# Half of the second chunk's first layer between parts of the first chunk's second layer, with the second group's joins and the third chunk's state later

## The chip, the cores and the metric

One core of one Trainium2 chip. The metric is the time of the kernel on the device in microseconds (us); lower is better. All timed runs here are of the fast state (for one single look the state is unknown). The kernel before took 670.79 us (median of 6 runs beside the changed kernel; 670.61 to 671.75).

## The reference, cut to what matters

```python
# deltanet: 4 batches x 8 heads, 768 steps, head size 48
for t in range(S):
    y[:, :, t] = einsum('bhd,bhde->bhe', q[:, :, t], state)
    v_old = einsum('bhde,bhd->bhe', state, k_n[:, :, t])
    state = state + b_t * einsum('bhd,bhe->bhde', k_n[:, :, t], v_t - v_old)
# then a feed-forward layer with exact Gelu, 3072 tokens
x = y.transpose(0, 2, 1, 3).reshape(B * S, H * D)      # 3072 x 384
return gelu(x @ w_in) @ w_out                          # 384 -> 2048 -> 384, w_* are float64 inputs
```

The kernel cuts the 768 steps into 12 chunks of 64. A group is two chunks. For a group VectorE eliminates a small triangular system ("elimination"), TensorE and VectorE join its halves ("joins"), then each chunk's state step gives x, its transpose xT, and the feed-forward work on it. The weights arrive as 64-bit floats and are decoded to 32 bits by integer work on VectorE and ScalarE.

## The kernel before: the parts that matter

The order of work is a plan. Each step has a time in units of one chunk of feed-forward work; steps are emitted in that order. VectorE keeps the emitted order (the kernel emits this plan under manual_schedule for VectorE alone); the queues of the other engines are ordered by a scheduler that follows it.

```python
    def back(x):                                  # end of the elimination: VectorE transposes
        if x == 0: transpose(XM <- Nu)            # L453
        else:                                     # L457: x == 1 right columns, x == 2 left columns
            transpose(Zf[:, :, cols] <- Nu)
        if x == 2:                                # clear two quarter blocks of Zf
            ...nc.scalar.mul / nc.gpsimd.memset   # L464, L466
    # ... cut ...
    def fc1(c, f):                                # first layer, one of 16 blocks of hidden units
        psH = ps.tile([128, NA * 128], F32, tag="mlp", name="psH")
        for m in range(NM):
            nc.tensor.matmul(psH, lhsT=w_in_sb[...], rhs=xTs[c][:, m, :], ...)
        nc.scalar.activation(G[:, f, :], psH, ACT.Gelu)

    def fc2(u, f0, f1):                           # second layer, four blocks f of one half of the tokens
        if f0 == 0: u.psO = ps.tile([128, DM], F32, tag="mlp", name="psO")
        for f in range(f0, f1):
            nc.tensor.matmul(u.psO, lhsT=G[:, f, ...], rhs=w_out_sb[:, f, :], ...)
    # ... cut ...
    ones = [(1.3, fc1, c, f) for f in range(NF)]
    twos = [(2.7, fc2, tiles[c, a], f, f + 4) for a in range(NA) for f in range(0, NF, 4)]
    if c == 0: twos.sort(key=lambda s: s[3])
    return ones + twos
    # ... cut ...
    plan = [at(c + 1, c + 2, ffn_steps(c)) for c in range(NC)]
    plan += [at(0.985, 1.26, decode_steps(3, n_in)), at(1.26, 1.65, decode_steps(n_in, NW)), ...]
    plan += [..., at(1.75, 2.45, eliminate_steps(1)),
             at(2.58, 2.74, join_steps(1)), at(2.72, 2.98, state_steps(2)), ...]
```

join_steps(1) are three steps: the first makes psJ from XM and G for the third chunk, and VectorE multiplies it into XM; the second makes the other half of the third chunk from Zf and the new XM, together with the first half of the fourth chunk; the third makes the rest.

Of the kernel before, what the change touches and what calls it, by code (L numbers as in the profile page):

```python
# [16 lines left out]
def kernel(  # L17
# [33 lines left out]
    NC = S // C  # L51
# [370 lines left out]
    def eliminate_steps(g):  # L422
        steps = []

        def scales():
            gt = wk.tile([128, HB], F32, tag="gt", name="gt", bufs=1)
            gl = XMs[g] = wk.tile([128, NU, HB], F32, tag="XM", name="XM", bufs=1)
            nc.vector.transpose(gt, gms[g].rearrange("q t h -> q (t h)"))
            nc.gpsimd.tensor_tensor(gl, low, gt.unsqueeze(2).to_broadcast([128, HB, HB]),
                                    op=ALU.mult)  # L430

        def flip():
            Nus[g] = wk.tile([128, HB, HB], F32, tag="Nu", name="Nu", bufs=1)
            nc.vector.transpose(Nus[g], Ds[g].rearrange("q u n -> q n u"))
            nc.vector.tensor_tensor(Nus[g], Nus[g], XMs[g], op=ALU.mult)

        def eliminate(j):
            nu = Nus[g]
            n = HB - 1 - j
            tmp = wk.tile([128, HB * HB // 4], F32, tag="tmp", name="tmp")  # L440
            tmp = tmp[:, 0:n * j].rearrange("q (i c) -> q i c", i=n)
            nc.vector.tensor_tensor(tmp, nu[:, j + 1:, j:j + 1].to_broadcast([128, n, j]),  # L442
                                    nu[:, j:j + 1, 0:j].to_broadcast([128, n, j]), op=ALU.mult)
            nc.vector.tensor_tensor(nu[:, j + 1:, 0:j], nu[:, j + 1:, 0:j], tmp, op=ALU.add)  # L444

        def diagonal():
            flat = Nus[g].rearrange("q i c -> q (i c)")
            nc.vector.memset(flat[:, 0:HB * HB:HB + 1], 1.0)

        def back(x):  # L450
            nu = Nus[g]
            if x == 0:
                nc.vector.transpose(XMs[g].rearrange("q u c -> q c u"),  # L453
                                    nu.rearrange("q i c -> q c i"))
            else:
                cols = slice(HB, C) if x == 1 else slice(0, HB)
                nc.vector.transpose(Zf[g % 2][:, :, cols].rearrange("q u i -> q i u"), nu)  # L457
            if x == 2:
                for cc in range(2):
                    for p in range(2):  # L460
                        part = Zf[g % 2][p * C + HB:(p + 1) * C,
                                         cc * NU // 2:(cc + 1) * NU // 2, 0:HB]
                        if g == cc == p == 0:
                            nc.scalar.mul(part, low[0:HB, 0:HB // 2], 0.0)  # L464
                        else:
                            nc.gpsimd.memset(part, 0.0)  # L466

        steps = [(0.3, scales), (3.0, flip)]
        steps += [(0.7, eliminate, j) for j in range(1, HB - 1)]
        steps += [(0.1, diagonal)]  # L470
        steps += [(1.9, back, x) for x in range(3)]
        return steps

    def join(g, ts, level, copy=nc.scalar.copy):

        xm, zf, off = XMs[g], Zf[g % 2], Gs[g]
        gm = gms[g].rearrange("q t h -> q (t h)")
        psJ = dn("psJ").rearrange("q b (u n) -> q b u n", n=HB)
        for i, u in enumerate(range(ts[0] * H, (ts[-1] + 1) * H)):
            for p in range(2):  # L480
                top = slice(p * C, p * C + HB)
                low_ = slice(p * C + HB, (p + 1) * C)
                rows, to = (top, low_) if level == 0 else (low_, top)
                nc.tensor.matmul(psJ[to, i // (2 * H), i % (2 * H), :],
                                 lhsT=(xm if level else off)[rows, u, :],
                                 rhs=zf[rows, u, HB:C] if level else xm[rows, u, :],
                                 start=True, stop=True)
        for i in range(0, len(ts), 2):
            us = slice(ts[i] * H, (ts[min(i + 1, len(ts) - 1)] + 1) * H)
            n = us.stop - us.start  # L490
            for p in range(2):
                top = slice(p * C, p * C + HB)
                low_ = slice(p * C + HB, (p + 1) * C)
                if level == 0:
                    nc.vector.tensor_tensor(
                        xm[low_, us, :], psJ[low_, i // 2, 0:n],
                        gm[low_, us].unsqueeze(2).to_broadcast([HB, n, HB]), op=ALU.mult)
                else:
                    copy(zf[top, us, HB:C], psJ[top, i // 2, 0:n])
# [43 lines left out]
    def join_steps(g):  # L543
        a, b = range(NA), range(NA, 2 * NA)
        return [(1.0, join_run, g, a, ()), (1.0, join_run, g, b, a), (1.0, join_run, g, (), b)]
# [120 lines left out]


    FH = NF // 2
    DH = DM // 2
    B11, B12 = w_out_sb[:, 0:FH, 0:DH], w_out_sb[:, 0:FH, DH:]  # L670
    B21, B22 = w_out_sb[:, FH:, 0:DH], w_out_sb[:, FH:, DH:]
    T = {}

    def fc1(c, f):
        psH = ps.tile([128, NA * 128], F32, tag="mlp", name="psH")
        for m in range(NM):
            nc.tensor.matmul(psH, lhsT=w_in_sb[:, f // 2, m, f % 2 * 128:(f % 2 + 1) * 128],  # L677
                             rhs=xTs[c][:, m, :], start=(m == 0), stop=(m == NM - 1))
        nc.scalar.activation(G[:, f, :], psH, ACT.Gelu)  # L679
# [112 lines left out]
    def ffn_steps(c):  # L792
        ones = [(1.3, fc1, c, f) for f in range(NF)]
        if c > 1:
            return [(1.3, first_layer, c, f) for f in range(NF)] + [
                (2.6, second_layer, c, n) for n in (1, 5, 2, 6, 4, 7, 3)]
        twos = [(2.7, fc2, tiles[c, a], f, f + 4) for a in range(NA) for f in range(0, NF, 4)]
        if c == 0:
            twos.sort(key=lambda s: s[3])
        return ones + twos  # L800

    def at(first, last, steps):

        total, done, timed = sum(s[0] for s in steps), 0.0, []
        for w, *step in steps:
            timed.append((first + (last - first) * (done + 0.5 * w) / total, step))
            done += w
        return timed
# [32 lines left out]
    signs(0, 2)  # L841
    diagonals(first[3])
    root(n0)
    scales_, flip_, *rows, back0, back1, back2 = [s_[1:] for s_ in eliminate_steps(0)]
    factors(gms[0], beta_m[:, 0:2].rearrange("q c a h -> q (c a) h"), n0)
    scales_[0]()
    flip_[0]()
# [36 lines left out]
    back2[0](*back2[1:])  # L884
    for a in range(NA):
        join(0, (a,), 1)
    for u in first[NA:]:
        scale_v(u)
    begin(0)
# [27 lines left out]
    def late():  # L917
# [3 lines left out]
        for a in range(NA):  # L921
# [3 lines left out]
            for c in range(5, NC, 2):  # L925
                tiles[c, a].Kb = Kb

    plan = [at(c + 1, c + 2, ffn_steps(c)) for c in range(NC)]
    plan += [at(0.985, 1.26, decode_steps(3, n_in)), at(1.26, 1.65, decode_steps(n_in, NW)), at(1.66, 1.67, [(1.0, late)])]
    plan += [at(0.98, 0.985, [(1.0, load, 3)]),  # L930
             at(1.02, 1.1, [(1.0, join, 0, range(NA, 2 * NA), level) for level in range(2)]),
]
    sums = [(1.0, sum_of_squares, tiles[c, a], h) for c in (2, 3) for a in range(NA) for h in range(H)]
    plan += [at(1.08, 1.5, sums), at(1.51, 1.511, [(1.0, prep, c) for c in (2, 3)]), at(1.65, 1.655, [(1.0, finish_both)]), at(2.97, 2.971, [(1.0, finish, 4)]), at(2.675, 2.676, [(1.0, queries, third)]),
             at(1.12, 1.6, state_steps(1)),
             at(1.75, 2.45, eliminate_steps(1)),
             at(2.58, 2.74, join_steps(1)), at(2.72, 2.98, state_steps(2)),
             at(2.67, 2.671, [(1.0, prep, 4)]), at(2.8, 2.9, [(1.0, grams, [tiles[4, a] for a in range(NA)])])]
    plan += [at(0.995, 1.0, [(1.0, load_v, 2)]), at(2.98, 2.981, [(1.0, sums_of_w)]), at(3.1, 3.11, [(1.0, last_sum_of_w)])]
    plan += [at(c - 0.4, c - 0.3, v_steps(c)) for c in range(4, NC)]  # L940
    plan += [at(2.08, 2.44, [(1.0, scale_head, tiles[c, a], h)
# [2 lines left out]
    for c in range(4, NC):  # L944
        us = [tiles[c, a] for a in range(NA)]
        t = {4: 1.8, 5: 2.1}.get(c, c - 2.9)
        plan += [at(t, t + 0.01, [(1.0, load_blocks, c, "Kb", k)])]
        t = 3.2 if c == 4 else c - (1.3 if c % 2 == 0 else 0.9)
        plan += [at(t, t + 0.01, [(1.0, load_blocks, c, "Qb", q)])]
        t = c - (2.1 if c % 2 == 0 else 2.6) if c > 5 else {4: 2.1, 5: 2.69}[c]  # L950
        plan += [at(t, t + 0.01, [(1.0, load_k, c, "Kn")])]
        plan += [at(c - 0.4, c - 0.39, [(1.0, load_k, c, "Kp")])]
        t = {4: 2.73, 5: 2.95}.get(c, c - (1.97 if c % 2 == 0 else 2.36))
        plan += [at(t, t + 0.01, [(1.0, turned_k, u) for u in us])]
        t = c + (0.05 if c % 2 == 0 else -0.34)
        plan += [at(t, t + 0.01, [(1.0, turned_q, u) for u in us])]
# [56 lines left out]
```

## Time and profile before

| what | before |
|---|---|
| time, median of 6 | 670.79 us |
| profiled execution | 671.82 us, span 670.1 us |
| TensorE busy, of the span | 640.3 us, 96% |
| VectorE busy, of the span | 452.3 us, 67% |
| end of weight decoding on VectorE | 117.3 us |
| first layer of the second chunk done | 141.22 us |
| first layer of the third chunk starts | 178.55 us |

The lines behind this table are shown in the prediction. To read them: a row of a timeline has start, length, engine, line, operation, output <- input, count, and in brackets how long the engine sat idle before and what ended it. "x24" records of psH are four steps of the first layer; each step is six records. Only time lost before about 230 us can be won; after that TensorE is busy 436.1 of 440.0 us (230 to 670), and its longest gap before its last record, at 666 us, is 0.12 us.

### The profile page before, as it was taken

How to read it: one execution, taken by the hardware profiler on the slowest of the kernel's cores; microseconds unless marked ns; L12 is line 12 of the kernel's file. 1: busy time of each engine (PE TensorE's matmuls, PEld its weight loads, DVE VectorE, ACT ScalarE, POOL GpSimd, SP SyncE). 2: the span in 40 equal slices, each digit the busy share in tenths (PEclk: the TensorE clock that was granted, in tenths of full speed). 3: DMA queues.
4: the chain of work that ended last, by engine and by line, in shares of the span. 5: the costliest groups of instructions: out<-in, count | busy, mean ns of one | idle time of the engine just before them, and what ended most of it. 6: DMA issues, size and time to landing. Idle time of an engine off the chain costs nothing.

```text
span 670.1 us, 21705 instructions
## 1 busy us (share of the span) xinstructions
PE 640.3 (96%) x9542; PEld 559.4 (83%) x9542; DVE 452.3 (67%) x921; ACT 228.6 (34%) x605; POOL 82.1 (12%) x82
## 2 busy tenths in 40 slices
PE   5767998999999999999999999999999999999997
PEld 4656775866689989989989989989989989989997
DVE  6999999994689846489846479846479844324021
ACT  3357754714342143142143142143142133122220
POOL 4051300103111021111021111021111010000000
PEclk8576999999999999999999999999999999999999
DMA  9785655203431232511332511211401210100101
GB/s 130 174 253 167 121 172 135 48 0 66 81 51 32 53 53 44 82 31 30 55 49 49 84 29 26 53 21 30 68 3 24 55 20 3 24 2 2 24 1 25
DMA packets 158431, 39.76 MB, mean 59 GB/s; under 512 B 150016, under 2 KB 153216, under 8 KB 158336
## 3 DMA queue, kind: packets, MB, share of 16 engines
q1 hardware_dynamic: 152464, 33.40, 26.3%
q10 hardware_dynamic: 5872, 4.97, 3.2%
q8 instruction: 75, 1.23, 0.8%
q14 instruction: 20, 0.16, 0.1%
HBM read 33.62 MB, written 4.72 MB: 57 GB/s over the span
## 4 chain that ended last, share of the span: by engine, by line
PE 82%; DVE 10%; ACT 3%; issue 2%; DMA 2%; SPq 1%; DVEq 0%; ACTq 0%
PE psH L677 36%; PE psX L715 12%; PE psY L715 12%; PE psZ L715 4%; PE psJ L517 3%; PE psK L572 3%; PE psG L367 3%; PE psO L690 2%; PE psU L597 2%; DVE Nu L444 2%; DVE tmp L442 2%; PE psY L615 1%; DVE w_e L235 1%; DVE w_out_sb L236 1%; PE psY L624 1%
## 5 line engine op out<-in xcount | busy, mean ns | idle before, releaser
L677 PE MATMUL psH<-xT,w_in_sb 128*128 128x256 f32 x1152 | 261.5, 383 | 2.3 <-ACT G L679 2.3
L677 PEld LDWEIGHTS psH<-xT,w_in_sb 128*128 128x128 f32 x1152 | 215.6, 190 | 33.7 <-ACT G L679 3.9
L679 ACT ACTIVATE G<-psH 128x256 f32<-128x256 f32 x192 | 73.3, 382 | 180.4 <-PE psH L677 168.3
L444 DVE TENSOR_TENSOR Nu<-Nu,tmp 128x30 f32<-128x30 f32 (+9 forms) x180 | 61.8, 343 | 6.2
L442 DVE TENSOR_TENSOR tmp<-Nu 128x30 f32<-128x30 f32 (+9 forms) x180 | 61.6, 342 | 5.1
L715 PE MATMUL psX<-w_out_sb,G 128*128 128x192 f32 x320 | 56.2, 329 | 0.0
L715 PE MATMUL psY<-w_out_sb,G 128*128 128x192 f32 x304 | 54.1, 329 | 0.6
L715 PEld LDWEIGHTS psX<-w_out_sb,G 128*128 128x128 f32 x320 | 52.2, 190 | 0.7
L715 PEld LDWEIGHTS psY<-w_out_sb,G 128*128 128x128 f32 x304 | 49.1, 190 | 2.1 <-DVE u L761 1.8
L690 PE MATMUL psO<-w_out_sb,G 128*128 128x384 f32 x128 | 45.1, 495 | 1.6 <-DVE w_out_sb L236 1.6
L660 ACT COPY xT<-psX 128x384 f32<-128x384 f32 x24 | 11.3, 476 | 102.9 <-PE psX L659 102.8
L306 POOL TENSOR_TENSOR n<-n,half 128x16 f32<-128x16 f32 x10 | 29.4, 2938 | 87.9 <-DVE n L281 66.9
L690 PEld LDWEIGHTS psO<-w_out_sb,G 128*128 128x128 f32 x128 | 23.1, 190 | 16.9 <-DVE w_out_sb L236 4.0
L603 ACT COPY U<-psU 64x192 f32<-64x192 f32 x96 | 30.0, 313 | 19.5 <-PE psU L597 18.3
L402 DVE TENSOR_TENSOR P<-psG,mask 128x1024 f32<-128x1024 f32 x10 | 12.2, 1224 | 35.6 <-PE psG L367 35.6
L580 DVE TENSOR_TENSOR W<-psK,V 128x384 f32<-128x384 f32 x22 | 12.1, 552 | 29.1 <-ACT y L579 29.0
L466 POOL MEMSET Zf<- 32x512 f32 x23 | 12.4, 541 | 154.5 <-DVE Zf L457 153.6
L724 DVE TENSOR_TENSOR S<-G 128x512 f32<-128x512 f32 x20 | 13.7, 687 | 25.8 <-ACT G L679 25.7
L332 POOL TENSOR_TENSOR V<-V,n 128x384 f32<-128x384 f32 x18 | 17.1, 958 | 106.1 <-DMA V<-in_v_dram 67.6
L638 DVE TENSOR_TENSOR x<-psY,y 64x192 f32<-64x192 f32 x80 | 28.3, 354 | 0.9
L715 PE MATMUL psY<-T,G 128*128 128x192 f32 x160 | 28.2, 329 | 0.0
L715 PE MATMUL psX<-T,G 128*128 128x192 f32 x160 | 28.1, 329 | 0.0
(138 smaller groups left out, 866.9 us busy)
## 6 DMA issues: line engine op xcount, KB each, us to landing
Kp<-in_k_dram SPq DMA_DIRECT2D x76, 96.0 KB, 3.6
w_out_sb<-in_moe_w_in_dram SPq DMA_DIRECT2D x24, 256.0 KB, 4.2
V<-in_v_dram SPq DMA_DIRECT2D x48, 96.0 KB, 2.9
out_dram<-o_sb ACTq DMA_DIRECT2D x46, 96.0 KB, 2.2
w_raw<-in_moe_w_out_dram SPq DMA_DIRECT2D x10, 384.0 KB, 5.4
Zf<-in_moe_w_out_dram SPq DMA_DIRECT2D x6, 384.0 KB, 5.1
Qp<-in_q_dram SPq DMA_DIRECT2D x64, 32.0 KB, 2.2
Qp<-in_q_dram SPq DMA_DIRECT2D x16, 96.0 KB, 4.3
```

Of the source, the lines that this page charges most:

```text
L306: nc.gpsimd.tensor_tensor(flat, flat, half, op=ALU.pow)
L367: nc.tensor.matmul(psG[HALF[p], r, i * NP + j, :], lhsT=u.Kt[rows, p, j, :], rhs=(u.Qt if x else u.Kt)[rows, p, j, :], start=True, stop=True)
L442: nc.vector.tensor_tensor(tmp, nu[:, j + 1:, j:j + 1].to_broadcast([128, n, j]), nu[:, j:j + 1, 0:j].to_broadcast([128, n, j]), op=ALU.mult)
L444: nc.vector.tensor_tensor(nu[:, j + 1:, 0:j], nu[:, j + 1:, 0:j], tmp, op=ALU.add)
L517: nc.tensor.matmul(psJ[to, i, :], lhsT=(xm if level else off)[rows, u, :], rhs=zf[rows, u, HB:C] if level else xm[rows, u, :], start=True, ...
L572: nc.tensor.matmul(u.psK[to, x, r, j, :], lhsT=(u.Qt if x else u.Kt)[rows, p, j, :], rhs=St[rows, u.a, p, j, :], start=True, stop=True)
L603: copy(pairs(u.U[HALF[p]], s), u.psU[HALF[p ^ s], p])
L638: nc.vector.tensor_tensor(dst, src, pairs(u.y[HALF[p ^ s]], s), op=ALU.add)
L677: nc.tensor.matmul(psH, lhsT=w_in_sb[:, f // 2, m, f % 2 * 128:(f % 2 + 1) * 128], rhs=xTs[c][:, m, :], start=(m == 0), stop=(m == NM - 1))
L679: nc.scalar.activation(G[:, f, :], psH, ACT.Gelu)
L690: nc.tensor.matmul(u.psO, lhsT=G[:, f, u.a * 128:(u.a + 1) * 128], rhs=w_out_sb[:, f, :], start=(f == 0), stop=(f == NF - 1))
L715: nc.tensor.matmul(ps_, lhsT=lhs[:, f, :], rhs=rhs[:, f, :], start=first and f == 0, stop=f == FH - 1, skip_group_check=not first)
```

## The change

Its intent: while TensorE waits for decoded second-layer weights of the first chunk, it does half of the second chunk's first layer. TensorE is then ahead, so what follows from VectorE's elimination is put later. Apart from that, two quarter blocks of the first group are cleared after the join copies and not before. The core of the diff:

```diff
-            if x == 2:
+            if x == 2 and g > 0:
+                clear(g)
+        def clear(g): ...                      # as before, for g == 0 called after join(0, (a,), 1)
+    EARLY = 8
     def fc1(c, f):
-        psH = ps.tile([128, NA * 128], F32, tag="mlp", name="psH")
+        if c == 1 and f < EARLY:
+            psH = dn("psH")[:, 0, 0:NA * 128]
+        else:
+            psH = ps.tile([128, NA * 128], F32, tag="mlp", name="psH")
@@ ffn_steps
-        return ones + twos
+            more_ = [(1.3, fc1, 1, f) for f in range(EARLY)]
+            return ones + twos[:-2 * NA] + more_[:4] + twos[-2 * NA:-NA] + more_[4:] + twos[-NA:]
+        return ones[EARLY:] + twos
@@ plan
-    plan = [at(c + 1, c + 2, ffn_steps(c)) for c in range(NC)]
+    plan = [at(c + 1 + 0.25 * (c == 1), c + 2 + 0.25 * (c == 0), ffn_steps(c)) for c in range(NC)]
-    queries of the third chunk at 2.675, joins at(2.58, 2.74), state at(2.72, 2.98), prep 4 at 2.67
+    queries of the third chunk at 2.725, joins at(2.64, 2.77), state at(2.76, 2.985), prep 4 at 2.72
-    load_k 5 at 2.69, turned_k 4 at 2.73 and 5 at 2.95
+    load_k 5 at 2.74, turned_k 4 at 2.76 and 5 at 2.955
```

(The last four lines stand for five lines of the diff in which only these numbers change; other lines are cut.)

More of the change, by code (lines that the diff above doesn't have):

```diff
@@ L457, in back, with clear @@
                 nc.vector.transpose(Zf[g % 2][:, :, cols].rearrange("q u i -> q i u"), nu)
-            if x == 2:
+            if x == 2 and g > 0:
+                clear(g)
+        def clear(g):
                 for cc in range(2):
@@ L471, in eliminate_steps @@
         steps += [(1.9, back, x) for x in range(3)]
-        return steps
+        return steps + [(0.0, clear, 0)] if g == 0 else steps
     def join(g, ts, level, copy=nc.scalar.copy):
@@ L843 @@
     root(n0)
-    scales_, flip_, *rows, back0, back1, back2 = [s_[1:] for s_ in eliminate_steps(0)]
+    scales_, flip_, *rows, back0, back1, back2, clear_ = [s_[1:] for s_ in eliminate_steps(0)]
     factors(gms[0], beta_m[:, 0:2].rearrange("q c a h -> q (c a) h"), n0)
@@ L886 @@
         join(0, (a,), 1)
+    clear_[0](*clear_[1:])
     for u in first[NA:]:
@@ L933 @@
     sums = [(1.0, sum_of_squares, tiles[c, a], h) for c in (2, 3) for a in range(NA) for h in range(H)]
-    plan += [at(1.08, 1.5, sums), at(1.51, 1.511, [(1.0, prep, c) for c in (2, 3)]), at(1.65, 1.655, [(1.0, finish_both)]), at(2.97, 2.971, [(1.0, finish, 4)]), at(2.675, 2.676, [(1.0, queries, third)]),
+    plan += [at(1.08, 1.5, sums), at(1.51, 1.511, [(1.0, prep, c) for c in (2, 3)]), at(1.65, 1.655, [(1.0, finish_both)]), at(2.97, 2.971, [(1.0, finish, 4)]), at(2.725, 2.726, [(1.0, queries, third)]),
              at(1.12, 1.6, state_steps(1)),
              at(1.75, 2.45, eliminate_steps(1)),
-             at(2.58, 2.74, join_steps(1)), at(2.72, 2.98, state_steps(2)),
-             at(2.67, 2.671, [(1.0, prep, 4)]), at(2.8, 2.9, [(1.0, grams, [tiles[4, a] for a in range(NA)])])]
+             at(2.64, 2.77, join_steps(1)), at(2.76, 2.985, state_steps(2)),
+             at(2.72, 2.721, [(1.0, prep, 4)]), at(2.8, 2.9, [(1.0, grams, [tiles[4, a] for a in range(NA)])])]
     plan += [at(0.995, 1.0, [(1.0, load_v, 2)]), at(2.98, 2.981, [(1.0, sums_of_w)]), at(3.1, 3.11, [(1.0, last_sum_of_w)])]
@@ L949 @@
         plan += [at(t, t + 0.01, [(1.0, load_blocks, c, "Qb", q)])]
-        t = c - (2.1 if c % 2 == 0 else 2.6) if c > 5 else {4: 2.1, 5: 2.69}[c]
+        t = c - (2.1 if c % 2 == 0 else 2.6) if c > 5 else {4: 2.1, 5: 2.74}[c]
         plan += [at(t, t + 0.01, [(1.0, load_k, c, "Kn")])]
         plan += [at(c - 0.4, c - 0.39, [(1.0, load_k, c, "Kp")])]
-        t = {4: 2.73, 5: 2.95}.get(c, c - (1.97 if c % 2 == 0 else 2.36))
+        t = {4: 2.76, 5: 2.955}.get(c, c - (1.97 if c % 2 == 0 else 2.36))
         plan += [at(t, t + 0.01, [(1.0, turned_k, u) for u in us])]
```

## The prediction

> **What bounds the kernel now.** I read the page first, then the chain of waits, then TensorE's own order of work, then busy time by stage. The page has TensorE at 96% of the span, and its second part shows that what is missing is at the start.
>
> ```profile
> PE   5767998999999999999999999999999999999997
> DVE  6999999994689846489846479846479844324021
> ```
>
> One digit is 16.75 us. From the seventh slice on TensorE is at 9 everywhere, so nothing after about 230 us can be won by moving work; there every microsecond won earlier is only carried along. VectorE is at 9 through slices two to nine, about 17 to 150 us: that is where another engine than TensorE sets the pace. Busy time in stretches that I cut at the joints of the feed-forward work (columns: length, then PE, PEld, DVE, ACT, POOL busy with counts, granted clock, DMA share, GB/s):
>
> ```profile
> 93.40:106.06 12.66, 12.44 (x55) 7.97 (x53) 12.45 (x18) 6.01 (x13) 0.00 (x0) 1.00 0.76 221
> 106.06:120.20 14.14, 12.55 (x39) 6.73 (x38) 13.80 (x21) 5.52 (x12) 1.56 (x1) 1.00 0.41 87
> 120.20:141.20 21.00, 20.99 (x98) 18.08 (x97) 19.02 (x53) 12.20 (x45) 0.36 (x1) 1.00 0.21 36
> 141.20:178.50 37.30, 35.17 (x793) 22.99 (x791) 23.19 (x44) 11.97 (x27) 8.60 (x7) 1.00 0.31 53
> 178.50:227.70 49.20, 48.85 (x652) 44.56 (x653) 44.86 (x97) 14.60 (x36) 4.58 (x5) 1.00 0.29 47
> ```
>
> The first two rows are the first chunk's second layer (psO), the third the second chunk's first layer (psH), the fourth the second chunk's second layer with the joins of the second group and the third chunk's state between its parts. The reader should compare PEld in rows one and two with row three: 8.0 of 12.7 and 6.7 of 14.1 against 18.1 of 21. The weight loads show how thin the work is where "busy" still says nearly full. TensorE's order of work says why:
>
> ```profile
> 106.06 4.04 PE L690 MATMUL psO<-w_out_sb,G 128*128 128x384 f32 x12
> 110.26 2.85 PE L690 MATMUL psO<-w_out_sb,G 128*128 128x384 f32 x8 [0.17 <-DVE w_out_sb L236]
> 114.05 2.85 PE L690 MATMUL psO<-w_out_sb,G 128*128 128x384 f32 x8 [0.94 <-DVE w_out_sb L236]
> 117.38 2.85 PE L690 MATMUL psO<-w_out_sb,G 128*128 128x384 f32 x8 [0.47 <-DVE w_out_sb L236]
> ```
>
> Each pair of second-layer weight blocks is decoded on VectorE (L218, L228, L230, L235, L236), one pair per 3.8 us (L236 starts at 105.45, 109.25, 113.04, 116.36), and TensorE uses a pair up in 8 records. The chain of waits is all VectorE up to there, and TensorE after it:
>
> ```profile
> 116.36 0.97 DVE w_out_sb L236
> 117.33 0.04 issue
> 117.38 2.85 PE psO L690 x8
> 120.22 2.59 PE psH L677 x12
> 122.82 18.40 PE psH L677 x84
> 141.22 5.16 PE psO L690 x16
> ```
>
> From it come the two rates that I use: psO 5.16/16 = 0.3225 us a record, psH 18.40/84 = 0.22 us a record.
>
> [...] VectorE-paced until 117 us, TensorE-paced after. [...] ScalarE sits 4.29 us before its L923 at 117.40. [...] The two psO accumulators of the first chunk hold both "mlp" banks, so an interleaved psH needs another place; the change takes it from "dn", two buffers whose last users (psU, psY of the second chunk) are done at about 105.
>
> **The change part by part.**
>
> (1) It removes no instruction. Eight of sixteen first-layer steps of the second chunk (48 psH records, 48 x 0.22 = 10.56 us) move from after 120.2 us to between the first chunk's psO steps: four after the parts f 0 to 7, four after f 8 to 11. They need xT of the second chunk (its copies start at 106.07, 0.83 us) and first-layer weights decoded by 85.5: ready as TensorE gets there. From 106.06 the old order had 36 psO records: 36 x 0.3225 = 11.61 us of work in 120.22 - 106.06 = 14.16 us, so 2.55 us were lost waiting for the decoder. New: 11.61 + 10.56 = 22.17 us, and 0.6 for four more changes between kinds of work, estimated at 0.15 each from the small gaps at such joints. The last psO parts then come after 122 us, five later than the last decode, so no wait is left. Half the first layer is done 22.8 us after the start instead of 14.16 + 10.56 = 24.7, a gain of 1.9.
>
> (2) Clearing the first group's quarter blocks later. Before, ScalarE clears (0.63 us at 47.68, after VectorE's second transpose) and only then copies the joins (1.51 us), so psU starts at 49.16. Now the copies run while VectorE transposes, as psJ is ready at about 46 and 47, and the clear comes last, at 47.7 to 48.3, with GpSimd's first memset until about 48.4. psU starts near 48.45: 0.7 us earlier. Does it travel? psU, U, x and xT hang on each other in the chain, and VectorE's wait of 0.91 us at 59.60 (for ScalarE's L223 at 58.62, behind those copies) shrinks to 0.2. VectorE then has hardly a gap until 117, so decode and all after it move 0.7 us: last decode at 116.6.
>
> (3) So the first layer of chunk two ends at 141.2 - 1.9 - 0.7 = 138.6.
>
> (4) Then joins and state. Work in 141.22 to 178.55: 64 psO x 0.3225 = 20.64; 256 psJ at 1.13 per 64 = 4.52; 146 psG at 1.09 per 64 = 2.49; psK 2.01; psU 1.12; psY 2.02; 6 psX x 0.11 = 0.66; sum 33.46 of 37.33 us. Lost: 3.87, of which 2.1 are waits that the trace names (0.59, 0.62, 0.28, 0.61), and the rest joints. VectorE's elimination for this group moves only by 0.7: its transpose XM at 143.88 to 145.98 becomes ready at 145.3, and the rest of L457 at 148.8. TensorE in the old order would reach the first join at 138.6 + 5.2 = 143.8 and wait 1.5. That is what the later times are for: with one more second-layer step before it, it arrives at 138.6 + 7.8 = 146.4, with no wait. The second join needs L525 (1.39 us after 148.8, so 150.2); it depends on one psO step of 2.6 being placed between. The state of chunk three has slack: psY ran at 171.14 though U was copied at 167.33, 3.8 us earlier. I expect about half of the 2.1 us of named waits to go: 1.1.
>
> Sum: 1.9 + 0.7 + 1.1 = 3.7 us; 671.0 - 3.7 = 667.3.
>
> **The rivals.**
>
> *ScalarE's queue turns the gain round.* Its L923 (two new Kb buffers, in memory freed by the decoder) cannot run before the last decode, and in the old kernel nothing useful stood behind it. If the new Gelus stand behind it, the two "dn" buffers are filled by 110.0, and TensorE stands until 117.9. Then 36 psH (7.9), 32 psO (10.3), joints 0.6 and the second half 10.56 follow: end at 147.3, six later than before, near 676. [...] Against: the queues are ordered by when work can start (transposes of the second chunk are woven between psO records in the trace), which would put the Gelus first.
>
> *The third chunk's state becomes the bound.* VectorE gained only 0.7, and if the third chunk's xT comes only 0.7 earlier, the result is 670.3. Against: the slack of 3.8 us. A milder form is likelier: ScalarE's square at 176.49 stands before the xT copy at 176.92, and it uses keys that landed at 174.80 after SyncE had issued eleven block loads ahead of them. If that load does not move, the third chunk's first layer starts about 176.3, a gain of 2.2: 668.8.
>
> *It is given back later.* In 178.5 to 227.7 VectorE is busy 44.86 of 49.2. But its elimination is done with XM at 233.67, and TensorE joins at 236.96: 3.3 us to spare, and VectorE's start there hangs on TensorE's psY anyway. I expect no giving back.
>
> *It goes better.* If all losses between 93 and 178 us went (0.9 + 2.55 + 3.87) and the 0.7 besides, it would be 8.0 us: 663. Joints don't vanish, so at most two thirds: 665.7.
>
> **Range and chances.** 667.3 us, 8 times in 10 between 664.8 and 669.9: the low end has most of the named waits gone, the high end has the state chain bind. Faster by 2% would take 13.4 us, more than all that is lost, so 0.01; slower by 2% needs double the worst rival, 0.01; within 2%, 0.98.
>
> **What would show it right or wrong.** Right: psH records between psO records from about 107 us; no psO wait for L236 after 110; L499 copies ahead of the clear and psU at about 48.5; L236 last near 115.7 to 116.6; the second half of the first layer done near 138.6; first join near 146 with no wait; third chunk's psH near 174.8; equal lengths from there on. Wrong: TensorE waiting for a Gelu near 110 to 118 (first rival); joins or xT no earlier than before (second); a new wait near 237 (third). The prediction as a whole falls if the time is over 670, or under 664.8.

## The result, and the profile after

The changed kernel takes 667.75 us (median of 6; 667.44 to 669.31). The ratio of the mean time of its fast runs to the mean time of the fast runs of the kernel before in the same rounds is 0.9956, 95% interval 0.9943 to 0.9969; it is not quite the ratio of the medians. At the 2% threshold that is "same", with a clear gain of about 3 us, where 3.7 was predicted.

Line numbers have moved: psH is L684 (was L677), psO L697 (L690), psJ L520 (L517), VectorE's product with psJ L528 (L525).

TensorE's order of work, to be held against the four psO lines in the prediction:

```profile
105.49 1.46 PE L697 MATMUL psO<-w_out_sb,G 128*128 128x384 f32 x4
106.78 5.34 PE L684 MATMUL psH<-xT,w_in_sb 128*128 128x256 f32 x24
111.96 5.32 PE L697 MATMUL psO<-w_out_sb,G 128*128 128x384 f32 x16
117.12 5.34 PE L684 MATMUL psH<-xT,w_in_sb 128*128 128x256 f32 x24
122.30 5.32 PE L697 MATMUL psO<-w_out_sb,G 128*128 128x384 f32 x16
127.46 10.52 PE L684 MATMUL psH<-xT,w_in_sb 128*128 128x256 f32 x48
137.82 7.90 PE L697 MATMUL psO<-w_out_sb,G 128*128 128x384 f32 x24
```

No line has a bracket: the decoder's waits are gone, and each row starts before the last one's modelled end (the second at 106.78, the first ends at 105.49 + 1.46 = 106.95), so no cost of changing between kinds of work shows here. From the start of the first row to the end of the first layer (the next psO starts at 137.98 in the chain of waits) it is 137.98 - 105.49 = 32.49 us; before it was 141.22 - 106.06 = 35.16. That is 2.67 us won.

The later clear, in ScalarE's timeline, before and after:

```profile
47.68 0.63 ACT L464 ACTIVATE Zf<-low 32x512 f32<-32x512 f32 x1 [3.95 <-DVE Zf L457]
48.32 1.51 ACT L499 COPY Zf<-psJ 32x256 f32<-32x256 f32 x4
```

```profile
45.54 0.73 ACT L502 COPY Zf<-psJ 32x256 f32<-32x256 f32 x2 [1.46 <-PE psJ L487]
46.42 0.74 ACT L502 COPY Zf<-psJ 32x256 f32<-32x256 f32 x2 [0.15 <-PE psJ L487]
47.23 0.63 ACT L467 ACTIVATE Zf<-low 32x512 f32<-32x512 f32 x1
```

The copies now lie under VectorE's transpose, and only the clear is left behind it. Of the shift between these two traces 0.45 us is not the change's: VectorE's L453 that ends the first elimination starts at 39.94 before and 39.49 after, with the same work ahead of it. So I measure below from that instruction.

Then the joins and the state. Before, TensorE's four waits over 0.15 us in this stage were these:

```profile
151.06 0.18 PE L517 MATMUL psJ<-Zf,XM 32*32 32x32 f32 x1 [0.59 <-issue]
154.80 1.04 PE L367 MATMUL psG<-Qt,Kt 48*64 48x64 f32 x54 [0.62 <-issue]
174.34 0.55 PE L659 MATMUL psX<-ident,x 128*128 128x128 f32 x3 [0.28 <-DVE x L638]
177.44 0.55 PE L659 MATMUL psX<-ident,x 128*128 128x128 f32 x3 [0.61 <-ACT xT L660]
```

TensorE's timeline of the changed kernel:

```profile
145.65 2.21 PE L520 MATMUL psJ<-XM,G 32*32 32x32 f32 x128
147.80 1.56 PE L697 MATMUL psO<-w_out_sb,G 128*128 128x384 f32 x4
150.52 1.20 PE L520 MATMUL psJ<-Zf,XM 32*32 32x32 f32 x64 [1.17 <-issue]
151.65 2.32 PE L697 MATMUL psO<-w_out_sb,G 128*128 128x384 f32 x4
153.90 1.97 PE L367 MATMUL psG<-Qt,Kt 48*64 48x64 f32 x64
```

TensorE reaches the first join at 145.65 without waiting, as foreseen, but waits 1.17 us before the second. "issue" says that the profile shows no releaser; VectorE's timeline names one all the same:

```profile
143.32 2.11 DVE L453 STREAM_TRANSPOSE XM<-Nu 128x1024 f32<-128x1024 f32 x1
145.32 3.68 DVE L457 STREAM_TRANSPOSE Zf<-Nu 128x1024 f32<-128x1024 f32 x2
149.03 2.82 DVE L528 TENSOR_TENSOR XM<-psJ,gm 32x512 f32<-32x512 f32 x4
```

The first two L528 end about 1.4 us after 149.03, that is at 150.4, and psJ starts at 150.52. The two rows after the wait are slow besides: four psO in 2.32 us (1.56 elsewhere) and 64 psG in 1.97 (1.16 elsewhere). The granted clock (the third number from the end) fell in the same stretch:

```profile
152.00:154.00 2.00, 2.00 (x8) 0.63 (x10) 0.89 (x2) 1.52 (x3) 0.96 (x1) 0.58 0.04 8
154.00:156.00 2.00, 2.00 (x76) 1.90 (x78) 0.06 (x1) 1.04 (x3) 1.93 (x1) 0.57 0.49 91
```

These four microseconds at 0.57 lose, if TensorE's work goes as the clock, 4 x 0.43 = 1.7 us; that is an estimate, and the two slow rows together took 0.76 + 0.81 = 1.57 us longer. And this execution was indeed the slowest of its six, 669.31 against a median of 667.75. The first layer of the third chunk starts at 176.07 (178.55 before), and the rest of the program takes the same in both: 667.6 - 176.07 = 491.5 and 670.1 - 178.55 = 491.5. All of the difference is made before it and none is given back later.

One caution for all that follows: a trace is one execution, not the median. The traced execution of the kernel before took 671.82 us, 1.0 above its median, and the first one of the changed kernel is 1.6 above its own. So differences of half a microsecond between two traces can be chance.

### The profile page after: what moved, and what is told of

It reads as the page before. It is cut to its first block, busy times and chain, and to the rows that moved or that the text cites. A ratio compares the mean times of both kernels' runs of the same rounds, so it can differ in the third digit from the quotient of the medians.

```text
span 667.6 us, 21705 instructions
## 1 busy us (share of the span) xinstructions
PE 643.4 (96%) x9542; PEld 563.6 (84%) x9542; DVE 451.9 (68%) x921; ACT 228.5 (34%) x605; POOL 82.3 (12%) x82
## 4 chain that ended last, share of the span: by engine, by line
PE 86%; DVE 7%; ACT 3%; issue 2%; DMA 1%; SPq 0%; DVEq 0%
PE psH L684 36%; PE psX L722 12%; PE psY L722 12%; PE psO L697 5%; PE psZ L722 4%; PE psK L575 3%; PE psJ L520 3%; PE psG L367 3%; PE psU L600 2%; PE psY L618 2%; DVE Nu L444 2%; DVE tmp L442 2%; PE psY L627 1%; ACT U L606 1%; PE psX L662 1%
## 5 line engine op out<-in xcount | busy, mean ns | idle before, releaser
L684 PE MATMUL psH<-xT,w_in_sb 128*128 128x256 f32 x1152 | 261.4, 383 | 2.4 <-ACT G L686 2.3
L684 PEld LDWEIGHTS psH<-xT,w_in_sb 128*128 128x128 f32 x1152 | 215.7, 190 | 33.7 <-ACT G L686 3.5
L697 PE MATMUL psO<-w_out_sb,G 128*128 128x384 f32 x128 | 45.0, 498 | 0.0
L697 PEld LDWEIGHTS psO<-w_out_sb,G 128*128 128x128 f32 x128 | 23.7, 191 | 14.4 <-DVE w_out_sb L236 0.6
```

Of the source, the lines that this page charges most:

```text
L684: nc.tensor.matmul(psH, lhsT=w_in_sb[:, f // 2, m, f % 2 * 128:(f % 2 + 1) * 128], rhs=xTs[c][:, m, :], start=(m == 0), stop=(m == NM - 1))
L697: nc.tensor.matmul(u.psO, lhsT=G[:, f, u.a * 128:(u.a + 1) * 128], rhs=w_out_sb[:, f, :], start=(f == 0), stop=(f == NF - 1))
```

## The experiments

Twelve runs in four sets, all correct. Times are medians. For comparing traces I use the time from the start of the first group's L453 to the start of the third chunk's first layer, which leaves out the chance in the start: before it is 178.55 - 39.94 = 138.61 us.

**Undo the later clear** (in the changed kernel):

```diff
-            if x == 2 and g > 0:
+            if x == 2:
-    clear_[0](*clear_[1:])
```

> The changed kernel with one part undone: the first group's quarter blocks are cleared before the join copies again. Prediction's step 2 (the later clear is worth 0.7 us): 668.4 to 668.5 us, ratio to before about 0.9966. Rival, read from the two traces (psU starts 0.75 us earlier for its first 9 records but then takes 2.59 instead of 1.96 us, and its copies follow only 0.1 us earlier once a 0.45 us shift that is there before the clear is taken off): 667.8 to 667.9, no difference that five rounds can see.

Measured 668.37 us, ratio 0.996 (0.9948 to 0.9973). The changed kernel's interval overlaps it, so the times alone don't settle it. The traces do better: from the first group's L453 to the end of decoding (VectorE's L265) it is 77.35 us here and 77.30 in the kernel before, and in the eleven traces of kernels with the later clear and unshifted work (all others but the last run) 76.60 to 77.20, mean 76.86. So it is worth 0.1 to 0.7 us, 0.5 in the mean. VectorE's wait for L223 (0.91 us at 59.60 before) goes with it: it is 0.34 to 0.36 us in seven of the eleven traces. In the other four it is 0.52 to 0.88, and there TensorE's psU, which starts earlier, takes 2.2 to 2.6 us instead of 2.0.

**The old times for joins and state** (in the changed kernel):

```diff
-  joins at(2.64, 2.77), state at(2.76, 2.985), ...
+  joins at(2.58, 2.74), state at(2.72, 2.98), ...
```

> The changed kernel with the old times for the second group's joins, the queries, the third chunk's state, its loads and transposes. Theory: the later times are needed because TensorE is 2.7 us ahead while VectorE's elimination is not; with the old times the first join stands after two psO steps and TensorE waits there about 1.5 to 2.3 us for XM (with more if the granted clock falls after the wait): 669.3 to 670.3 us. Rival: TensorE's queue is ordered so that other work fills the wait, or the state only starts later now and gains nothing: 667.5 to 668.0.

Measured 670.35 us, ratio 0.999 (0.9977 to 1.0003): nearly the whole gain is gone. TensorE's timeline:

```profile
137.32 5.32 PE L697 MATMUL psO<-w_out_sb,G 128*128 128x384 f32 x16
144.96 1.20 PE L520 MATMUL psJ<-XM,G 32*32 32x32 f32 x64 [2.31 <-DVE XM L453]
```

What the moved steps won (2.67 us) is lost again, nearly all of it, in one wait for VectorE's XM. The rival, that other work fills the wait, is out.

**A later second transpose** (in the changed kernel):

```diff
-             at(1.75, 2.45, eliminate_steps(1)),
+             at(1.75, 2.41, eliminate_steps(1)[:-1]), at(2.665, 2.666, eliminate_steps(1)[-1:]),
```

> The changed kernel plus one move on VectorE: of the second group's two transposes into Zf (L457, 1.84 us each) the second, which only psU needs, comes after the first join's two L528. Theory: the wait of 1.17 us before psJ<-Zf at 150.52 is VectorE's L528 standing behind both transposes, so it vanishes, and with it the fall of the granted clock to 0.58 in the 4 us after it: 666.4 to 666.8 us, and the clock stays at 1.00 from 150 to 156. Rival: the join waits for something else (a buffer, the queue of ScalarE), or the third chunk's state takes the time back: 667.5 to 667.9.

Measured 667.59 us, ratio 0.9952 (0.994 to 0.9963): no gain beyond noise. The wait before psJ<-Zf is gone, so the reading of "issue" there as a wait for L528 behind both L457 was right. But a new gap of 0.63 us stands before the last three psK records. The time went with the rival.

**Four moved steps instead of eight:**

```diff
-    EARLY = 8
+    EARLY = 4          # and 0.1226 in place of 0.25 in the plan
```

> Four instead of eight first-layer steps of the second chunk moved forward (24 psH records, 5.2 us, all after the parts f 0 to 7). Theory: what is won is the 2.55 us of waiting for the weight decoder, and 5.2 us of other work already covers that (f 12, 13 are decoded at 112.5, f 14, 15 at 115.8, and TensorE gets to them at 117.1): same as the changed kernel, 667.4 to 668.0 us. Rival: the gain goes with the amount moved, so half of it comes: 669.2 us.

Measured 667.55 us, ratio 0.995 (0.9937 to 0.9963): the same as with eight. The gain does not go with the amount moved.

**The changed kernel again:**

> The changed kernel itself once more, to stand beside the others of this set: 667.4 to 668.1 us, ratio to before 0.9956 give or take 0.001. In the profiled execution of the first time the granted clock fell to 0.58 from 152 to 156 us after a wait of 1.17 us; if that belongs to the schedule it comes again, if it is chance it need not.

Measured 667.9 us, ratio 0.996 (0.9947 to 0.9973). The wait of 1.15 us is there, the fall of the clock is not (1.00 from 150 to 160 us). So the fall of the clock is chance, not a property of the schedule (of the three traces of this kernel, after, after_again and after_third, one has it); the wait is a property (1.17, 1.15 and 1.15 us). This trace is the undisturbed one: 173.51 - 39.10 = 134.41 us to the third chunk.

**Only the later clear:**

```diff
 (the kernel before, with the clear of the first group after join(0, (a,), 1))
```

> The kernel before with only the later clearing of the first group's quarter blocks. Prediction's step 2: 0.7 us, 670.1. Rival: 0.1 us, 670.7. From the first set (the changed kernel lost 0.6 in the median when this was undone, and from the end of the elimination to the end of decoding the traces show 77.3, 77.35 without it and 77.2, 77.1, 76.7, 76.6 with it) I expect 0.3 to 0.6: 670.2 to 670.5.

Measured 669.93 us against 670.53, but ratio 0.9998 (0.9984 to 1.0012), with two of its six runs at 671.4 and 671.5: not to be told from nothing by time.

**The later clear and the later times, no moved steps:**

```diff
 (the kernel of clear_only)
-  joins at(2.58, 2.74), state at(2.72, 2.98), ...
+  joins at(2.64, 2.77), state at(2.76, 2.985), ...
```

> The kernel before with the later clear and the later times for joins and state, but without the moved first-layer steps. With clear_only, the first set's run with the old times, and the changed kernel it makes a square of two by two. Theory: the later times have nothing to win where TensorE is not ahead; only the wait of 0.59 us before the second join can go: 669.9 to 670.5. Rival: the later times are worth the same 2.6 us here as they were in the changed kernel: 667.8.

Measured 668.9 us, ratio 0.9977 (0.9965 to 0.9989), better than I expected: the later times are worth about 1.4 us (0.9998 - 0.9977 = 0.0021 of 670.5; with both intervals, 0.2 to 2.6) even where TensorE is not ahead. Its TensorE timeline shows why:

```profile
140.10 7.90 PE L693 MATMUL psO<-w_out_sb,G 128*128 128x384 f32 x24
147.94 2.21 PE L520 MATMUL psJ<-XM,G 32*32 32x32 f32 x128
150.08 1.56 PE L693 MATMUL psO<-w_out_sb,G 128*128 128x384 f32 x4
151.57 1.20 PE L520 MATMUL psJ<-Zf,XM 32*32 32x32 f32 x64
```

There is no wait at all in these rows. In the clear_only trace the waits of this stage are 0.62, 0.47, 0.27 and 0.28 us, 1.64 in all, much as in the kernel before; with the later times only 0.18 is left. The joins had stood too early in the old kernel already: the 0.62 is the wait before the second join. (The 0.47 is taken up with the last experiment.)

With the changed kernel this makes a square (all with the later clear; ratio to the kernel before, and the time from L453 to the third chunk in the trace):

| | old times | later times |
|---|---|---|
| no moved steps | 0.9998, 137.39 us | 0.9977, 136.06 us |
| eight moved steps | 0.9990, 136.61 us | 0.9953 to 0.996, 134.41 and 135.00 us |

The two traces of the last field (after_again, after_third) differ by 0.6 us, all of it before the end of decoding. Counted from there (the end of VectorE's L265) to the third chunk, the square is 60.50 and 59.10 us above, 59.81 and 57.64 (57.63) below. So the moved steps bring 0.7 us with the old times and 1.5 with the later ones, though they save TensorE 2.7 us of waiting for the decoder in both.

**One moved step:**

```diff
-    EARLY = 8
+    EARLY = 1          # and 0.0307 in place of 0.25 in the plan
```

> One first-layer step (6 psH records, 1.3 us) moved forward instead of eight, all else as in the changed kernel. Theory: the gain is the decoder's wait that gets covered, up to 2.55 us: half of it is covered, TensorE still waits about 1.2 us before psO: 668.8 to 669.2 us. Rival one, gain by the amount moved: an eighth of it, 670.2. Rival two, the gain is made by the later times and not by the moved steps: 667.7.

Measured 668.26 us, ratio 0.9964 (0.9952 to 0.9976): 0.5 us below the range I expected. One step covers 1.3 us of the decoder's wait (0.47 us of it are left before the last psO). TensorE then reaches the second join later and does not wait there: 134.72 us to the third chunk, against 134.41 and 135.00 with eight. Counted from the start of the first chunk's last 36 psO records, the second chunk's first layer ends after 32.50 us with eight steps and 33.87 with one; most of these 1.37 us are the 1.15 that TensorE then waits before the second join.

**Once more: the changed kernel, the later transpose, and the later transpose with four steps:**

> The changed kernel once more, only to stand in the same rounds as the two that follow: 667.4 to 668.1 us. TensorE waits about 1.15 us before psJ<-Zf near 150 us, as in each of its traces.

> The kernel of the run split again (second transpose into Zf after the first join's L528). In its first profile the 1.15 us wait was gone but a gap of 0.63 us stood inside the psK records at 160 us, for which the profile names nothing. Theory: that gap is chance (other schedules show 0.32 or none there), the move is worth up to 1.1 us: 666.6 to 667.2 us. Rival: the gap follows from the move, or the state takes the rest back: 667.5, as measured the first time (0.2 better than the changed kernel).

> Both the later second transpose and four instead of eight moved steps. Theory: the number of moved steps does not matter from about two on, so the same as split_again within 0.3 us, 666.6 to 667.4; the best of all kernels here would be one of these two.

Measured 667.68 (ratio 0.9953, 0.994 to 0.9965), 668.5 (0.9956, 0.9944 to 0.9969) and 667.4 us (0.9945, 0.9932 to 0.9959). The later transpose is not worth 1.1 us; neither kernel with it beats the changed kernel beyond noise. The lowest median, 667.4, is that of split_early4, but its interval holds the others. Two lines of split_again show it:

```profile
149.61 1.20 PE L520 MATMUL psJ<-Zf,XM 32*32 32x32 f32 x64
160.45 0.32 PE L575 MATMUL psK<-St,Qt 48*64 48x48 f32 x3 [0.85 <-issue]
```

The second join starts without a wait, and 0.85 us are lost before the last three psK. In split_early4 it is 1.31 us, in early4 0.32, each time before the same record. Where the 1.15 us wait stands at the second join (after_again, after_third) this gap is not there. So the gap stands in all three traces with the move, in the place of the wait removed. But it isn't bound to the move: early4 has no later transpose, and has both a wait of 0.99 us at the second join and a gap of 0.32; clear_times and early1 have neither.

**Where does the gap belong?**

```diff
 (the kernel of split)
-            nc.tensor.transpose(psB[:, c - c0, :], ...)
+            for _ in range(2 if c0 == 2 else 1):
+                nc.tensor.transpose(psB[:, c - c0, :], ...)     # same values, written twice
```

> The kernel of split with ten transposes of the small beta block done twice near 12 us (same result, 10 more TensorE records and 10 more weight loads early in its stream; all later orders are the same). In split, split_again, split_early4 and early4 a gap that the profile puts to nothing stood before the third last of the 128 psK records near 160 us, always there. Theory: TensorE waits there for its own instructions, [...] so the gap belongs to a place in the stream: with 20 instructions more ahead of it, it stands ten psK records earlier, about 19 into the last 32 instead of 29. Rival: it belongs to that record (an operand, a buffer): it still stands before the last three, or is gone. The time is not the question: 667 to 669 us.

One look, 670.44 us, of unknown state. TensorE's timeline:

```profile
153.45 1.14 PE L520 MATMUL psJ<-Zf,XM 32*32 32x32 f32 x60
156.23 0.32 PE L520 MATMUL psJ<-Zf,XM 32*32 32x32 f32 x4 [1.64 <-issue]
```

The gap has left psK and stands before the last four records of the third join; the rival (it belongs to that record) is out. My number was wrong: I expected ten records earlier, and it is 4 + 8 + 125 = 137 records earlier, with their weight loads 274 instructions, and 275 with the one semaphore instruction between them. Without the 20 inserted instructions that is 255. The page of the changed kernel has a number beside it: its row of the instruction queue (packets, MB, share) is

```profile
q8 instruction: 75, 1.23, 0.8%
```

and in the packed trace each of the 75 packets is 16384 bytes. TensorE's stream in this trace has 19181 instructions, and 19181/75 = 255.7. So I estimate, from these two numbers and the 255 above, a stretch of 256 instructions to a packet. One stretch plus the 20 inserted instructions is 276, beside 275 counted: by this estimate the gap stands at a border between two stretches, one stretch earlier than before. The border where it stood in split has moved by ten records, as expected, but TensorE passes it without a gap.

The kept traces show what comes before the end of such a gap. Seven traces have one: before (the 0.62 us before psG), clear_only (the 0.47), early4, split, split_again, split_early4 and split_shift. They are 0.32 to 1.64 us long and stand between records that are each 32x32 or 48x64 weights. Counted in instructions, all seven stand at the same place in a stretch of 256, to within one. The traces also hold each packet of queue q8. If packets and stretches are matched in order, there are 1036 starts of a stretch in the 14 traces: none comes less than 1.22 us after its packet has ended, about 6 us is usual, and the seven gaps end 1.22 to 1.45 us after it. In split, for example, the packet ran from 157.78 to 158.65 and TensorE went on at 160.09. My reading of these times is that TensorE waits there for the packet that brings its next instructions. In clear_times and early1 the same stretch started 1.82 and 2.04 us after its packet, with a little to spare and no gap. A pause of 0.43 us inside the first psU of the first trace after stands at such a border too (1.39 us after the packet), and one of 0.27 us in split (1.33 us): in these traces the later clear won little. No run changed the packets themselves: the reading, and that a wait at the second join gives the packet time, so that no gap follows, are argued, not shown.

With the gap in split_shift the clock fell again (0.97, 0.50 and 0.67 in the three stretches of 2 us from 154 us). By the same estimate as above, 2 x (0.03 + 0.50 + 0.33) = 1.7 us, that makes up most of this run's longer time (670.44 against 667.59 in split). Over the traces: in three (after, times_back, split_shift) the granted clock fell to half for about 3.4 us, with a wait or gap of 1.17, 2.31 and 1.64 us; in five (after_again, after_third, clear_back, early4, split_early4), with waits or gaps of 0.99 to 1.31 us, it did not.

## Why the prediction was right, and where its steps were not

The time, 667.75 us, is within 0.5 us of the 667.3 predicted, and inside the range. But the terms of the sum moved in different directions.

- **Step 1, moved steps, 1.9 us.** The mechanism is as told: psH between psO from 106.8 us, no wait for L236 left. The size was too small: 2.67 us. The term that failed is "0.6 for four more changes between kinds of work": they cost nothing measurable (rows of 5.34 and 5.32 us follow each other without a gap).
- **Step 2, later clear, 0.7 us.** Right in its mechanism (copies ahead of the clear), and 0.5 us in the mean of eleven traces, 0.1 in the worst. VectorE's 0.91 us wait at 59.60 was to shrink to 0.2: it was 0.34 to 0.36 in seven of the eleven, but 0.88 in the first trace after. The first trace misled here: 0.45 us of its earlier psU are chance at the start.
- **Step 3**, the end of the first layer at 138.6: it was 137.98.
- **Step 4, joins and state, 1.1 us.** Here a part failed. The first join is reached at 145.65 without a wait, as predicted (146.4). But the second join "depends on one psO step of 2.6 being placed between", and only half a step was (four records, from 147.80, 1.3 us): TensorE waits 1.15 us for L528. The stage from the end of the first layer to the third chunk took 37.33 us before and 173.51 - 137.01 = 36.50 in after_again: 0.8 won, as the four old waits that vanish (2.10) less the new ones (1.15, and 0.18 before psY) would make. But clear_only, with the old order of this stage, took 36.69, and against that it is 0.2. In the first trace the fall of the clock hid it.
- **Readings of lines.** TensorE's row of slices is at 9 from the eighth slice on; the seventh is 8. Of the four "waits that the trace names" two have a name; the other two are "issue", and the 0.62 among them stands at such a border of the instruction stream, 1.42 us after the packet's end; the trace names no other engine for it. A psO record brings one weight load of 0.19 us in 0.3225 us, so at full rate psO shows 0.59 of PEld and psH 0.19/0.22 = 0.86: the first row of the table of stretches (0.63) isn't thin, only the second (0.48) is.
- **Rivals.** ScalarE's queue: out; the four Gelus ran from 108.67 to 112.46, ahead of the Kb copies at 116.85. The third chunk's state as the bound: out as it was told (its keys and squares did not hold xT up), but its root was right: VectorE had gained only about 0.5 us, so its elimination became the bound at the second join. Given back later: out, 491.5 us from the third chunk to the end in both. "It goes better": not reached.

So what carried the prediction was its cap: VectorE hardly moves, so TensorE cannot keep all of its 2.67 us. That the sum came out near is partly luck, a too small first term against two too large ones. Nor do the measured terms add up exactly: they make 3.4 to 4.0 us, and the medians differ by 3.0. They are read from single traces, that of the kernel before 1.0 us above its median and that of after_again 1.2 below its own.

## What to carry to other kernels

Moving work into an engine's wait won here no more than the next wait for the slower engine left: 2.7 us of waiting were covered, and 1.5 reached the third chunk. The move and the times of what follows had to be changed together; either half alone brought 0.5 and 1.4 us, both 2.5 to 3. When a wait that has been removed does not show in the time, look for the gap that has come in its place before making the removal larger.
